# The gate projection of the last two token groups by seven block products instead of eight

## The chip, the cores and the metric

The kernel runs on one core of one Trainium2 chip. The metric is the device time of one execution in microseconds. Before the change it is 318.22 us, the median of 3 runs (317.78 to 318.86). The execution that was profiled took 317.96 us, of which the profile's span, from the first to the last instruction, is 316.2 us.

## The reference

A linear attention (cosformer) of 8 batches, 8 heads, 576 positions and 64 dimensions is followed by a gated feed-forward block. The attention's output, 4608 tokens of 512 values, is the input of three weight matrices. Cut to what matters:

```
q_p, k_p = phi(q), phi(k)              # relu, times cos and sin of the position
kv  = einsum('bhsf,bhsd->bhfd', k_p, v);  z = sum_s k_p
x   = (q_p @ kv) / (q_p . z + 1e-6)    # 4608 x 512 after the heads are joined
g   = x @ w_gate                       # 512 x 1536
val = x @ w_val                        # 512 x 1536
out = (g * sigmoid(g) * val) @ w_out   # 1536 x 512
```

All inputs and the output are float32 in memory. The kernel works in bfloat16 and float16 with float32 sums.

## The kernel before

**Groups and slots.** The 4608 tokens are 36 tiles of 128 and 9 groups (0 to 8) of 512 tokens. The order of all instructions is written out by hand; no scheduler moves them, and each engine takes its own list in order. The feed-forward work of a group is the frame. It has 16 slots: 12 columns of 128 gate and value outputs (`ffn_fc`, `fc` 0 to 11) and 4 steps of the output projection. Behind each step `slot(s)` issues what was planned for that slot with `at(s, ...)`: attention of the next group's tiles, work on the next batches' q, k and v, and their loads.

**A column before.** `ffn_mm` (L535) makes 4 matmuls of 512 columns with `wg_sb` into one PSUM bank and 4 with `wv_sb` into another. ScalarE takes the silu of the gate bank (`ffn_silu`, L541), VectorE multiplies it with the value bank into `ht` (`ffn_mul`, L546). `ht` holds 12 columns of 512 tokens in fp16.

**The output projection.** From group 2 on, `out_by_quarters` (matmuls at L649) computes `ht @ w_out` as a 2 x 2 block product by seven products for eight: `weight_sum` (L614) made four sums of `w_out` blocks once, in group 1; `token_sum` (L623) makes four sums of `ht` blocks in each group, called behind columns 7 to 11 (`sums_behind`). ScalarE seeds a bank with a copy (L671), later matmuls add to what was put there, and VectorE makes the sums between banks (L679, L690). Results go to `ob` (L662 on ScalarE, L664 on VectorE) and to memory by SP's queue (`store`, L574; in the last group `store_two`, L581, on two queues).

**PSUM.** All 8 banks are one tile. `take` picks a bank when the program is written: among those that nobody holds, the one that was touched longest ago. `give_back` ends a hold in the program's text; on the chip the next writer of the bank still waits by semaphore until the last reader is done. For `"o"` banks, one whose neighbour is held is preferred, so that pairs stay whole for the attention tiles, which need two.

**Attention of later tiles.** `a_tile2` (L419) makes 16 or 8 small matmuls per half tile into two banks; VectorE then makes den, rec and x (L429, L438, L442); `x_turn` transposes x into `xT` by a DMA on SP's queue (L519). `relu_k` and `phi_q` (L238, L255), `vmul` (L259) and `kv_mm` (L305) prepare the next batch. Loads of q, k, v and weights are issued by POOL (`load`, L111) behind small copies that hold the queue.

Of the kernel before, what the change touches and what calls it, by code (L numbers as in the profile page):

```python
# [10 lines left out]
FP32 = mybir.dt.float32  # L11
# [3 lines left out]
ALU = mybir.AluOpType  # L15
# [3 lines left out]
def kernel(  # L19
# [28 lines left out]
    HC = FC // 2  # L48
    HT = T // 2
    HD = d_model // 2  # L50

    consts = ctx.enter_context(tc.tile_pool(name="consts", bufs=1))
    raw = ctx.enter_context(tc.tile_pool(name="raw", bufs=3))
    rel = ctx.enter_context(tc.tile_pool(name="rel", bufs=1))
    phip = ctx.enter_context(tc.tile_pool(name="phip", bufs=2))
    xp = ctx.enter_context(tc.tile_pool(name="xp", bufs=4))
    xtp = ctx.enter_context(tc.tile_pool(name="xtp", bufs=3))
    smp = ctx.enter_context(tc.tile_pool(name="smp", bufs=3))
    sgp = ctx.enter_context(tc.tile_pool(name="sgp", bufs=5))
    obp = ctx.enter_context(tc.tile_pool(name="obp", bufs=2))  # L60
    psum = ctx.enter_context(tc.tile_pool(name="psum", bufs=1, space=bass.MemoryType.PSUM))

# [10 lines left out]
    def take(n, hold=None, fills=False, seeded=False):  # L73

        taken = {x for r in held.values() for x in r}
        free = [b for b in range(0, 8, n) if not any(b <= x < b + n for x in taken)
                and (filled[b] or not seeded)]

        b0 = min(free, key=lambda b: (n == 1 and hold is not None and hold[0] == "o" and b ^ 1 not in taken,
                                      sorted(used[b:b + n], reverse=True)))  # L80
        if hold is not None:
            held[hold] = range(b0, b0 + n)
        filled[b0:b0 + n] = [fills or seeded] * n
        touch(range(b0, b0 + n))
        return banks[:, b0] if n == 1 else banks[:, b0:b0 + n]
# [15 lines left out]

    def raw_of(b, nm):
        if (b, nm) not in raws:
            raws[b, nm] = raw.tile([P, G, NC, D], BF16, name=f"raw_{nm}")
        return raws[b, nm]

    def load(b, nm, parts=1):
# [48 lines left out]
    ident = consts.tile([P, P], BF16)  # L156
    make_identity(nc, ident)
    kvd = []
    for j in range(2):
        t = consts.tile([P, 8 * J * D1], BF16, name=f"kvd_{j}")  # L160
        if j:
            nc.gpsimd.memset(t.bitcast(FP32), 0.0)
        kvd.append(t.rearrange("p (e j w i x) -> p e j w i x", e=2, j=J, w=2, i=2))


    zeros = consts.tile([P, P], BF16)
# [41 lines left out]
        in_=csk.rearrange("p c e -> p (c e)").to_broadcast([P, NC * 2, D]),  # L208
    )
    v2s = []  # L210
    for j in range(2):
        t = consts.tile([P, G, NC, 2, W], BF16, name=f"v2_{j}")
        nc.vector.tensor_copy(out=t[:, :, :, :, D], in_=csk.unsqueeze(1).to_broadcast([P, G, NC, 2]))
        v2s.append(t)


    wg_sb = consts.tile([P, KC, d_ff], BF16)
    wv_sb = consts.tile([P, KC, d_ff], BF16)
    wg_r = moe_w_gate.rearrange("(c p) f -> p c f", p=P)
    wv_r = moe_w_val.rearrange("(c p) f -> p c f", p=P)  # L220
    wo_r = moe_w_out.rearrange("(c p) f -> p c f", p=P)
# [35 lines left out]

    def vmul(b, g):
        nc.vector.tensor_tensor(  # L259
            out=v2s[b % 2][:, g, :, :, 0:D],  # L260
            in0=(first if b == 0 and g == 0 else {"v": raw_of(b, "v")})["v"][:, g].unsqueeze(2).to_broadcast([P, NC, 2, D]),
            in1=tab, op=ALU.mult,
        )
# [34 lines left out]
    def kv_mm(b):  # L298
        ps = st[b, "kvps"] = take(2, ("kv", b))
        for j, c in [(j, c) for j in range(J) for c in range(NC)]:  # L300
            for i in range(2):
                for e in range(2):
                    es = slice(e * SH, (e + 1) * SH)
                    g = 2 * j + i
                    nc.tensor.matmul(  # L305
                        out=ps[i * D:(i + 1) * D, e, j * 2 * D1:(j + 1) * 2 * D1],
                        lhsT=raws[b, "k"][es, g, c],
                        rhs=v2s[b % 2][es, g, c, :, 0:D1],
                        start=(c == 0), stop=(c == NC - 1),
                    )  # L310

# [47 lines left out]
            give_back(("kvf", j))  # L359


    qf = consts.tile([P, 2, J, 2, D], BF16)
    qr = [lodge(4 * J * SH, BF16).rearrange("p (e j c s) -> p e j c s", e=2, j=J, c=2) for i in range(2)]
    qwT = [lodge(8 * J * SH, BF16).rearrange("p (w e j c s) -> p w e j c s", w=2, e=2, j=J, c=2) for i in range(2)]

# [68 lines left out]
    def x_rec(t, ps, ys=slice(0, 4)):  # L434
        if ys.start == 0:
            st["rec", t] = smp.tile([P, H, 1], FP32, name="rec")
            st["x", t] = xp.tile([P, d_model], BF16, name="x")
        nc.vector.reciprocal(out=st["rec", t].rearrange("p (e y) o -> p e y o", e=2)[:, :, ys],  # L438
                             in_=st["den", t].rearrange("p (e y) o -> p e y o", e=2)[:, :, ys])

# [40 lines left out]
    def x_norm(t):  # L481
        num = st.pop(("num", t)).rearrange("p j e (i x) -> p (j e i) x", i=2)
        den = smp.tile([P, H, 1], FP32, name="den")
        nc.vector.tensor_scalar(out=den, in0=num[:, :, D:D1], scalar1=1e-6, scalar2=DOWN,
                                op0=ALU.add, op1=ALU.mult)
        rec = smp.tile([P, H, 1], FP32, name="rec")
        nc.vector.reciprocal(out=rec, in_=den)
        x = xp.tile([P, d_model], BF16, name="x")
        for j in range(J):
            hs = slice(4 * j, 4 * j + 4)  # L490
            nc.vector.tensor_tensor(
                out=x[:, 4 * j * D:(4 * j + 4) * D].rearrange("p (i e d) -> p e i d", i=2, e=2),
                in0=num[:, hs, 0:D].rearrange("p (e i) d -> p e i d", e=2),
                in1=rec[:, hs].rearrange("p (e i) o -> p e i o", e=2).to_broadcast([P, 2, 2, D]), op=ALU.mult,
            )
        st["x", t] = x

    def xT_of(t):
        tg, off = divmod(t, GH // 2)
        if tg not in xT:  # L500
            xT[tg] = xtp.tile([P, GH // 2, KC, P], BF16, name="xT")
        return xT[tg][:, off]

    def x_turn_pe(t, ks=slice(0, KC)):
        ps = take(1, ("xt", t, ks.start)).bitcast(BF16).rearrange("p (k x) -> p k x", x=P)
        for kc in range(ks.start, ks.stop):
            nc.tensor.transpose(out=ps[:, kc], in_=st["x", t][:, kc * P:(kc + 1) * P], identity=ident)  # L507
        st["xt", t, ks.start] = ps[:, ks]

    def x_turned(t, eng, ks=slice(0, KC)):  # L510
# [40 lines left out]
    def ffn_act(*a):  # L551
        ffn_silu(*a)
        ffn_mul(*a)

    def ffn_fc(*a):

        ffn_mm(*a)
        ffn_act(*a)

    out_v = out.rearrange("(b p c) f -> b c p f", p=SH, c=NC)  # L560
    o_ps = {}
# [68 lines left out]
    def out_by_quarters(tg, slot_of):  # L630
# [60 lines left out]
        if last:  # L691
            store_two(t0 + 2, slice(HD, d_model))
        product(c, aq[:, 1, 1], T4, False)
        copied("dve", C21, c)
        free("c")
        if last:
            store_two(t0 + 2, slice(0, HD))
# [178 lines left out]
    for b in range(2, B):  # L876
        s0 = SLOTS * (b - 1)
        keng = "dve" if b == 2 else "act"
        steps = [lambda b=b, g=g: phi_q(b, g) for g in range(G)]
        steps += [lambda b=b, g=g: (relu_k(b, g, g + 1, keng), vmul(b, g)) for g in range(G)]  # L880
        if b == 2:
            fs, tq = [s0 + i for i in (0, 0, 1, 1, 4, 5, 5, 6)], (s0 + 2, s0 + 2)
        else:
            p0 = s0 - SLOTS
            fs, tq = [p0 + 12, p0 + 12] + [p0 + 11 + i for i in range(2, 8)], (p0 + 15, p0 + 16)
            if b == 3:
                fs, tq = [p0 + 12 + i for i in range(4)] + [s0 + 4, s0 + 4, s0 + 5, s0 + 5], (s0 + 2, s0 + 2)
            at(p0 + 3 if b < 5 else p0 + 1, lambda b=b: load_behind(b))
        tk = (s0 + 4, s0 + {2: 8, 3: 7}.get(b, 5))
        for s, f in zip(fs, steps):  # L890
            at(s, f)
        for e in range(2):
            at(tq[e], lambda b=b, e=e: qturn_dma(b, e))
        at(tk[-1], lambda b=b: kv_mm(b), lambda b=b: kv_out2(b))
        at(tk[-1] + 1, lambda b=b: kv_free(b))
    for t in range(2 * OUT, NTG * OUT):
        tg, i = divmod(t, OUT)
        s = SLOTS * (tg - 1) + (5 if tg > 2 else 4) + 2 * i
        if t == 2 * OUT:
            at(s, a_(t, 0))  # L900
            at(s + 1, a_(t, 1), turn(t))
        elif tg == 2:
            at((9, 10, 11)[i - 1] + SLOTS, lambda t=t: a_tile2(t), turn(t))
            if i == 2:
                at(11 + SLOTS, load_3)
        else:
            if t in (13, 14, 15):
                s = SLOTS * 2 + t - 4
            at(s, lambda t=t: a_tile2(t), turn(t))
    for tg in range(1, NTG):  # L910
        s0 = SLOTS * tg
        for fc in range(FC):
            ffn_fc(tg, fc)
            if tg > 1:
                sums_behind(fc)
            slot(s0 + fc)
        if tg > 1:
            out_by_quarters(tg, lambda i: slot(s0 + FC + i))
            continue
        for i in range(OUT):  # L920
            ffn_out(tg * OUT + i)
            weight_sum(i)
            slot(s0 + FC + i)
# [31 lines left out]
```

## Time and profile before

| | before |
|---|---|
| time, median of 3 runs | 318.22 us (317.78 to 318.86) |
| profiled execution | 317.96 us, span 316.2 us |
| granted TensorE clock | 1.000 |
| TensorE busy | 309.1 us, 98% |
| VectorE busy | 220.2 us, 70% |
| ScalarE busy | 134.1 us, 42% |
| GpSimd (POOL) busy | 35.5 us, 11% |
| group 7, gate and value columns with attention tiles | 250.6 to 272.3 us |
| group 7, output projection | 272.3 to 281.5 us |
| group 8, gate and value columns | 281.5 to 302.2 us |
| group 8, output projection | 302.2 to 311.4 us |

PE is the matmul part of TensorE, PEld its weight loads, DVE is VectorE, ACT ScalarE, SP the engine whose queue issues most transfers. A row of the instructions in order of time gives the start, the time that the merged rows cover, engine, line, operation, out<-in, shape and count, and in brackets the idle time before it and what ended it. A matmul's duration runs beyond the start of the next, as they are pipelined; the distance of starts is what a stream costs.

### The profile page before, as it was taken

The numbers are of one execution on the slowest core, as the hardware profiler recorded it, in microseconds if no ns is written. First come the engines' busy times: TensorE is split into PE (matmuls) and PEld (weight loads), VectorE is DVE, ScalarE is ACT, GpSimd is POOL, SyncE is SP. The second block draws the span as 40 slices with busy tenths as digits, with TensorE's granted clock in tenths as the row PEclk, the third lists the DMA queues.
The fourth block names the chain that finished last, engine by engine and source line by source line (L and its number), as shares of the span: only waits on it lengthen the run. The fifth ranks groups of instructions, "written<-read, shape, count | busy, mean of one in ns | idle before, by whom it ended". The sixth has DMA issues, their size and how long they took to land.

```text
span 316.2 us, 6614 instructions
## 1 busy us (share of the span) xinstructions
PE 309.1 (98%) x2624; PEld 182.7 (58%) x2624; DVE 220.2 (70%) x441; ACT 134.1 (42%) x245; POOL 35.5 (11%) x60
## 2 busy tenths in 40 slices
PE   8899999999999999999999999999999999999994
PEld 4596555455445485548554765477456745774473
DVE  7873777797658888597858785879578437743652
ACT  7554545753435354335433453344433133213330
POOL 6754102000201100030003000300000000000000
PEclk9999999999999999999999999999999999999999
DMA  7999999998796985979795979598951241133004
GB/s 259 220 198 197 206 205 139 226 130 110 140 225 88 175 116 135 129 80 197 148 142 75 200 149 145 72 199 134 157 77 35 58 93 23 39 69 72 2 0 133
DMA packets 74766, 41.06 MB, mean 130 GB/s; under 512 B 49904, under 2 KB 69872, under 8 KB 74736
## 3 DMA queue, kind: packets, MB, share of 16 engines
q1 hardware_dynamic: 51952, 22.55, 39.7%
q0 software_dynamic: 22192, 17.57, 37.1%
q10 hardware_dynamic: 592, 0.52, 0.5%
q8 instruction: 20, 0.33, 0.4%
q14 instruction: 10, 0.08, 0.1%
HBM read 37.75 MB, written 9.44 MB: 149 GB/s over the span
## 4 chain that ended last, share of the span: by engine, by line
PE 86%; DVE 6%; DMA 4%; ACT 2%; issue 1%; DVEq 0%; ACTq 0%
PE banks L535 57%; PE banks L649 15%; PE banks L592 6%; DMA xT<-x 4%; PE banks L305 3%; PE banks L419 2%; DVE ht L546 1%; DVE sums L623 1%; DVE x L442 1%; PE banks L465 1%; PE banks L401 1%; DVE v L259 1%; PE banks L172 1%; PE banks L345 0%; PE banks L507 0%
## 5 line engine op out<-in xcount | busy, mean ns | idle before, releaser
L541 ACT ACTIVATE sg<-banks 128x512 bf16<-128x512 f32 (+2 forms) x116 | 65.8, 568 | 118.7 <-PE banks L535 115.6
L535 PE MATMUL banks<-xT,wg_sb 128*128 128x512 bf16 (+2 forms) x464 | 111.3, 364 | 0.3 <-DMA xT<-x 0.2
L535 PE MATMUL banks<-xT,wv_sb 128*128 128x512 bf16 (+2 forms) x464 | 111.3, 364 | 0.0
L546 DVE TENSOR_TENSOR ht<-sg,banks 128x512 f16<-128x512 bf16 (+2 forms) x116 | 74.5, 648 | 52.2 <-PE banks L535 45.5
L535 PEld LDWEIGHTS <-wv_sb 128*128 128x128 bf16 x464 | 44.9, 98 | 48.7
L535 PEld LDWEIGHTS <-wg_sb 128*128 128x128 bf16 x464 | 43.0, 98 | 42.3 <-issue 0.4
L649 PEld LDWEIGHTS <-ht 128*128 128x128 f16 x336 | 32.4, 98 | 3.9
L649 PEld LDWEIGHTS <-sums 128*128 128x128 f16 x252 | 24.6, 98 | 3.6 <-issue 0.8
L259 DVE TENSOR_TENSOR v<-raw_v,tab 128x1152 bf16<-128x1152 bf16 x31 | 22.7, 751 | 0.3 <-ACT raw_v L712 0.3
L592 PE MATMUL banks<-wo_sb,ht 128*128 128x512 f16 x96 | 22.7, 379 | 0.0
L442 DVE TENSOR_TENSOR x<-banks,rec 128x512 bf16<-128x512 f32 (+1 forms) x32 | 21.6, 674 | 1.3 <-PE banks L401 0.3
L649 PE MATMUL banks<-wo_sb,ht 128*128 128x256 f16 x168 | 20.6, 273 | 0.0
L649 PE MATMUL banks<-wt_sb,sums 128*128 128x256 f16 x168 | 19.5, 273 | 0.0
L649 PE MATMUL banks<-wt_sb,ht 128*128 128x256 f16 x168 | 19.5, 273 | 0.0
L255 DVE TENSOR_TENSOR r_q<-raw_q,tab 128x1152 bf16<-128x1152 bf16 x24 | 17.6, 752 | 2.4 <-ACT raw_q L238 2.1
L238 ACT ACTIVATE raw_k<-raw_k 128x576 bf16<-128x576 bf16 (+1 forms) x25 | 17.0, 694 | 0.0
L861 POOL COPY hold<-phit 1x2 bf16<-1x2 bf16 x5 | 1.2, 234 | 130.4 <-DMA phit<-r_q 130.4
L623 DVE TENSOR_TENSOR sums<-ht 128x1024 f16<-128x1024 f16 (+1 forms) x28 | 15.5, 552 | 0.2
L238 ACT ACTIVATE raw_q<-raw_q 128x576 bf16<-128x576 bf16 x24 | 15.0, 674 | 0.0
L592 PEld LDWEIGHTS <-ht 128*128 128x128 f16 x96 | 9.1, 98 | 8.9 <-issue 0.2
L419 PEld LDWEIGHTS <-phit 128*128 128x128 bf16 (+1 forms) x240 | 10.0, 100 | 6.5 <-issue 1.3
L664 DVE TENSOR_SCALAR ob<-banks 128x512 f32<-128x512 f32 (+1 forms) x15 | 9.8, 656 | 4.4 <-PE banks L649 3.6
(98 smaller groups left out, 223.9 us busy)
## 6 DMA issues: line engine op xcount, KB each, us to landing
out_dram<-ob SPq DMA_DIRECT2D x67, 128.0 KB, 2.4
raw_k<-in_k_dram POOLq DMA_DIRECT2D x7, 576.0 KB, 9.0
raw_q<-in_q_dram POOLq DMA_DIRECT2D x6, 576.0 KB, 6.5
raw_v<-in_v_dram POOLq DMA_DIRECT2D x6, 576.0 KB, 11.7
wo_sb<-in_moe_w_out_dram POOLq DMA_DIRECT2D x3, 512.0 KB, 12.8
wg_sb<-in_moe_w_gate_dram POOLq DMA_DIRECT2D x5, 256.0 KB, 9.0
wv_sb<-in_moe_w_val_dram POOLq DMA_DIRECT2D x5, 256.0 KB, 9.3
wo_sb<-in_v_dram SPq DMA_DIRECT2D x2, 576.0 KB, 4.1
```

Of the source, the lines that this page charges most:

```text
L238: nc.scalar.activation(out=out, in_=in_, func=AF.Relu)
L255: nc.vector.tensor_tensor(out=st[b, "q"][:, g], in0=o.unsqueeze(2).to_broadcast([P, NC, 2, D]), in1=tab, op=ALU.mult)
L259: nc.vector.tensor_tensor(out=v2s[b % 2][:, g, :, :, 0:D], in0=(first if b == 0 and g == 0 else {"v": raw_of(b, "v")})["v"][:, g].unsqueez ...
L419: nc.tensor.matmul(out=ps[ms, e, g * D1:(g + 1) * D1], lhsT=phit[b][:, e, g, c:c + n].rearrange("p c s -> p (c s)"), rhs=kv2s[b % 2][:, e, ...
L442: nc.vector.tensor_tensor(out=st["x", t].rearrange("p (y e d) -> p e y d", e=2, d=D)[:, :, ys], in0=ps[:, :, 0:2 * J * D1].rearrange("p e ...
L535: nc.tensor.matmul(out=st["f", tg, fc, lo][i], lhsT=(wg_sb, wv_sb)[i][:, kc, fs], rhs=xT[tg][:, ts, kc], start=(kc == 0), stop=(kc == KC - 1))
L541: nc.scalar.activation(out=sg[:, 0:n], in_=st["f", tg, fc, lo][0], func=AF.Silu, scale=DOWN)
L546: nc.vector.tensor_tensor(out=ht[:, fc, r:r + n], in0=st.pop(("s", tg, fc, lo))[:, 0:n], in1=ps[1], op=ALU.mult)
L592: nc.tensor.matmul(out=o_ps[t], lhsT=ht[:, fc, r:r + P], rhs=wo_sb[:, fc], start=(fc == 0), stop=(fc == FC - 1))
L623: nc.vector.tensor_tensor(out=o[:, lo:hi], in0=x[:, lo:hi], in1=y[:, lo:hi], op=op)
L649: nc.tensor.matmul(out=to[i][:, 0] if len(to) == 2 else to[0][:, i], lhsT=a[:, kc, i * P:(i + 1) * P], rhs=b[:, kc], start=first and kc == ...
L664: nc.vector.tensor_single_scalar(out=o_, in_=p_, scalar=x, op=ALU.mult)
```

## The change

The gate projection of groups 7 and 8 is computed block by block, 2 x 2 blocks, with seven products for eight, in the same form as the output projection. For each third `u` of the columns (4 columns of 128) the blocks are two halves of the 512 inputs and two halves of the 512 tokens.

- `ffn_by_quarters` replaces the 12 columns of `ffn_fc` in groups 7 and 8. A block product is 4 matmuls of 256 columns (L608 of the changed kernel). ScalarE seeds bank b with a copy of bank a (L636), copies the product e to `m7` in SBUF (L640); VectorE makes c = m7 + b in a bank (L646) and m7 = m7 + b (L655); ScalarE takes four silus of half columns (L614). The value columns stay 4 matmuls of 512 (L620), each into a bank of its own, and VectorE multiplies them with the gates (L625). The order of the columns is 0, 2, 1, 3, 4, 6, 5, 7, 8, 10, 9, 11.
- Sums: `gate_weight_sum` makes four sums of `w_gate` blocks into `wgs_sb`, one at the end of groups 1, 2, 4 and 5; `x_sum` (L592) makes four sums of `xT` blocks in slots 14 and 15 before each of the two groups. The sums of `ht` are called at other places in these groups.
- `take` prefers a bank whose neighbour is held also for names "g" and "v", while fewer than three pairs are whole.
- x, `xT` and the gate and value weights are fp16 in place of bf16; there is a second identity for it, made on POOL.
- Room: k and v have two raw buffers each in place of three; `v2_1` and `qf` lie in `wgs_sb` and serve only batches 0 and 1, so later batches all use `v2_0`; both `kvd` lie in one tile, which later holds the sums of x.
- C21 of the output projection is copied by ScalarE in place of VectorE, in all groups. Group 8's attention tiles stand in slots 1, 2, 5 and 6 of group 7 in place of 5, 7, 9 and 11.

```diff
-    raw = ctx.enter_context(tc.tile_pool(name="raw", bufs=3))
+    raw = ctx.enter_context(tc.tile_pool(name="raw", bufs=2))
+    rawq = ctx.enter_context(tc.tile_pool(name="rawq", bufs=3))
...
-        b0 = min(free, key=lambda b: (n == 1 and hold is not None and hold[0] == "o" and b ^ 1 not in taken,
+        whole = sum(b not in taken and b + 1 not in taken for b in range(0, 8, 2))
+        b0 = min(free, key=lambda b: (n == 1 and hold is not None and b ^ 1 not in taken and
+                                      (hold[0] == "o" or hold[0] in "gv" and whole < 3),
                                       sorted(used[b:b + n], reverse=True)))
...
+    ident16 = consts.tile([P, P], FP16)
+    make_identity(nc, ident16)
...
-            out=v2s[b % 2][:, g, :, :, 0:D],
+            out=v2s[b == 1][:, g, :, :, 0:D],
...
+    def gate_weight_sum(n):
+        o, x, y, op = ((W1, A21, A22, ALU.add), (W2, W1, A11, ALU.subtract), (W3, A11, A21, ALU.subtract),
+                       (W4, A12, W2, ALU.subtract))[n]
+        nc.vector.tensor_tensor(out=o, in0=x, in1=y, op=op)
...
+    def x_sum(tg, n):
+        B11, B12, B21, B22 = x_parts(tg)
+        o, x, y = ((X1, B12, B11), (X2, B22, X1), (X3, B22, B12), (X4, B21, X2))[n]
+        nc.vector.tensor_tensor(out=o, in0=x, in1=y, op=ALU.subtract)
+
+    def ffn_by_quarters(tg, slot_of):
...
+        def product(to, u, a, x, first):
+            for i in range(2):
+                for c in range(KH):
+                    nc.tensor.matmul(out=to[:, i], lhsT=a[:, c, 2 * u + i], rhs=x[:, :, c],
+                                     start=first and i == 0 and c == 0, stop=c == KH - 1, skip_group_check=True)
...
+        def V(u, i, w):
+            fc = 4 * u + 2 * i + w
+            val[u, i, w] = take(1, ("v", tg, fc), fills=True)
...
+        for u in range(3):
+            a = bank("a", fills=True)
+            product(a, u, A11, B11, True)
+            b = bank("b", seeded=True)
+            nc.scalar.copy(out=b, in_=a)
+            e = bank("e", fills=True)
+            product(e, u, W3, X3, True)
+            m7 = m7p.tile([P, 2, HT], FP32, name="m7")
+            nc.scalar.copy(out=m7, in_=e)
+            free("e")
+            V(*((u - 1, 1, 1) if u else (u, 0, 0)))
+            done()
+            product(b, u, W2, X2, False)
+            c = bank("c", seeded=True)
+            nc.vector.tensor_tensor(out=c, in0=m7, in1=b, op=ALU.add)
+            product(a, u, A12, B21, False)
+            silu(u, 1, 0, a)
+            free("a")
+            if u:
+                mul(u - 1, 1, 1)
+            V(u, 0, 0) if u else V(u, 1, 0)
+            done()
+            product(b, u, W1, X1, False)
+            nc.vector.tensor_tensor(out=m7, in0=m7, in1=b, op=ALU.add)
+            silu(u, 0, 1, m7)
+            product(c, u, A22, X4, False)
+            silu(u, 0, 0, c)
+            free("c")
+            V(u, 1, 0) if u else V(u, 0, 1)
+            done()
+            if u == 2:
+                for n in (1, 2):
+                    token_sum(n, 0, 4)
+            mul(u, 0, 0)
+            mul(u, 1, 0)
+            if u == 2:
+                token_sum(3, 4, 6)
+            product(b, u, W4, B22, False)
+            silu(u, 1, 1, b)
+            free("b")
+            if u:
+                V(u, 0, 1)
+            mul(u, 0, 1)
+            if u:
+                done()
+                token_sum(*((3, 0, 4) if u == 1 else (4, 0, 4)))
+        V(2, 1, 1)
+        mul(2, 1, 1)
+        for n in (1, 2):
+            token_sum(n, 4, 6)
+        done()
...
-        copied("dve", C21, c)
+        copied("act", C21, c)
...
+    for n in range(4):
+        at(SLOTS * (1 + n * (GATE[0] - 1) // 4) + FC + 3, lambda n=n: gate_weight_sum(n))
+    for tg in GATE:
+        for n in range(4):
+            at(SLOTS * (tg - 1) + FC + (2, 2, 3, 3)[n], lambda tg=tg, n=(2, 0, 1, 3)[n]: x_sum(tg, n))
...
+            elif tg - 1 in GATE:
+                s = SLOTS * (tg - 1) + ((1, 2, 7, 9) if tg < 6 else (1, 2, 4, 7) if tg < 8 else (1, 2, 5, 6))[i]
...
+        if tg in GATE:
+            ffn_by_quarters(tg, lambda i: slot(s0 + i))
+        for fc in range(FC) if tg not in GATE else ():
```

## The prediction

> **What bounds the kernel now.** I read the page's busy times first, then the chain that ended last, then TensorE's waits, and last the instructions in order of time for the stretch that the change rewrites.
>
> ```profile
> span 316.2 us, 6614 instructions
> PE 309.1 (98%) x2624; PEld 182.7 (58%) x2624; DVE 220.2 (70%) x441; ACT 134.1 (42%) x245; POOL 35.5 (11%) x60
> ...
> PEclk9999999999999999999999999999999999999999
> ...
> PE 86%; DVE 6%; DMA 4%; ACT 2%; issue 1%; DVEq 0%; ACTq 0%
> ```
>
> TensorE is busy 98% of the span at full clock, and 86% of the last chain is TensorE. Its end in order of time:
>
> ```profile
> 272.52 9.17 PE banks L649 x84
> 281.69 20.72 PE banks L535 x96
> 302.41 9.18 PE banks L649 x84
> 311.61 0.42 DVE ob L664
> ```
>
> One group of the last two is 96 matmuls (20.72 us) and 84 output matmuls (9.18 us), back to back. Only 4.6 us of the span lie behind the last matmuls. So a matmul saved there is time saved, and a wait of TensorE there is time lost. The rows in order of time give all prices:
>
> ```profile
> 276.28 1.47 PE L649 MATMUL banks<-wo_sb,ht 128*128 128x256 f16 x12
> 276.55 0.70 DVE L679 SCALAR_TENSOR_TENSOR banks<-ob,banks 128x512 f32<-128x512 f32 x1 [1.48 <-PE banks L649]
> ...
> 277.59 2.78 PE L649 MATMUL banks<-wt_sb,ht 128*128 128x256 f16 x24
> 277.79 0.60 ACT L662 ACTIVATE ob<-banks 128x512 f32<-128x512 f32 x1 [2.02 <-PE banks L649]
> ...
> 283.25 1.03 PE L535 MATMUL banks<-xT,wg_sb 128*128 128x512 bf16 x4
> 283.52 0.69 DVE L546 TENSOR_TENSOR ht<-sg,banks 128x512 f16<-128x512 bf16 x1 [1.10 <-PE banks L535]
> ...
> 284.11 1.03 PE L535 MATMUL banks<-xT,wv_sb 128*128 128x512 bf16 x4
> 284.31 0.60 ACT L541 ACTIVATE sg<-banks 128x512 bf16<-128x512 f32 x1 [1.13 <-PE banks L535]
> ```
>
> Starts matter more than durations here. Four 512-column matmuls take 284.11 - 283.25 = 0.86 us (20.72 / 96 = 0.216 each); twelve of 256 columns take 277.59 - 276.28 = 1.31 (0.109 each). ScalarE starts 0.20 us after the slot of the last matmul it needs ends (284.31 - 284.11), VectorE 0.27 (283.52 - 283.25). A silu lasts 0.60, a product or sum with a PSUM operand 0.69. So whoever waits for a silu of a bank gets it 0.80 us after the matmuls.
>
> **What goes.** Per group the gate part is 48 matmuls of 512 columns now and 3 x 7 x 4 = 84 of 256 then; the value part stays 48. That is 48 x 0.216 = 10.37 against 84 x 0.109 = 9.16: 1.2 us a group, 2.4 us in all. LDWEIGHTS (98 ns) stay under 109 ns. [...]
>
> **What comes on other engines, and why most is free.** Weight sums: 4 x 0.95 (row of L614, same shape) on VectorE, each at the end of the output part of groups 1, 2, 4 and 5, 2 and more groups ahead of use; it has 30% idle. Token sums of x: 4 x 0.42 a group (row of L623, 128x512). The first two run right after the output's C22 sum (L690, ends 279.79), where C21's copy stood, so X3 is there at 280.2 and needed 0.44 us after 281.52; their x tiles landed 2.4 us after an issue at 275.10. X1 and X2 come early too. C21's copy on ScalarE costs 0.60 where ScalarE waits 2 us (L662). Group 8's attention tiles move up from slots 5, 7, 9, 11 to 1, 2, 5, 6 with their transposes on SP's queue, which is empty there between 257 and 263 us. The extra identity on POOL, about 0.5 us by its rows (194 and 293 ns), stands before a copy that waits 1.8 us for the first v load, so POOL's queue of loads is not later. Two buffers for k and v: the load of k at 102.73 would reuse what the k/v products from 70.00 on read, 31 us earlier. One v2 tile: batch 3's writes, near 97 us, follow products that end at 71.2. fp16 for bf16: the fp16 output matmuls run at the same 0.216 (10.36 / 48 at L592). If that cover were gone: the weight sums cost up to 3.8, POOL 0.5, C21 0.6.
>
> **What comes on the path: the value matmuls' banks.** In the old loop a pair of banks comes round after four columns, some 7 us, and nobody waits. In the new one the choice of a bank changes: while fewer than three pairs are whole, a gate or value tile takes a bank whose neighbour is held. Right after `free("a")` that is bank a itself, whose silu has just been asked for, and after `free("c")` it is c. The value matmul behind it then waits for that silu, and all of TensorE behind it. Nothing in the trace of before shows this wait, but its parts are rows. I number time from group 7's first gate matmul, with 0.44 for a block product, 0.86 for a value column, 0.27 for an attention tile (8 small matmuls; 260.96 to 261.22 in this trace).
>
> Group 7, first third. Products a 0 to 0.44, e to 0.87, value column 0 to 1.74, b to 2.17, a to 2.61. Silu of a 2.81 to 3.41. Column 2 wants bank a: waits 3.41 - 2.61 = **0.80**, and ends 4.27. Attention tile to 4.54, b to 4.98, c to 5.41. VectorE takes the tile's three operations (rows 0.16, 0.20, 0.69) from 4.81 to 5.91 before it can do m7 + b, to 6.6; then silu of m7 to 7.2 and, behind it in ScalarE's queue, silu of c to 7.83. Column 1 wants bank c at 5.41: waits **2.4**.
> Second third. Column 1 ends 8.7, tile, b, a and e end 10.27. Column 3 gets the bank of column 1, whose multiplication is the last of three behind another tile's x: x ends 10.3, the three end 10.9, 11.6, 12.2. Waits **1.9**. Column 4 wants bank a again: **0.80**. Columns 6 and 5 find multiplied banks.
> Last third. Column 7 takes the bank of column 5: tile x, then three multiplications on VectorE, TensorE waits **0.75**. Columns 8 to 11 find free banks. In the output part the last two sums of ht stand behind this backlog: **0.4**. Small rest 0.1.
> Sum 0.80 + 2.4 + 1.9 + 0.80 + 0.75 + 0.5 = 7.2.
>
> Group 8 has no attention tiles. Column 2 **0.80**. Column 1 without the tile on either engine: c ends 1.3 after column 2, m7 + b ends 1.4 after b's 0.44 and 0.27 + 0.69, two silus (0.66 and 0.60) end 2.67 after column 2 and c is done at 0.87: **1.8**. Columns 4 and 8 behind silu of a: **0.80** each. Output part, last copies and sums behind multiplications: **0.4**. Sum 4.6.
>
> The bounds of the whole, if the waits are there at all (A below is the case without them): from below, each of the five waits for silu of a cannot be under 0.60, and the four others are between 0.7 (a single silu or multiplication, never less, as the bank's reader follows by program order) and the sums above: 3.0 + 2.8 = 5.8. From above, every such wait lengthened by the largest queue seen (one silu and one multiplication, 1.3): 11.8 + 4 x 1.3 = 17. I take 11.8, since each of its terms is a chain of rows of this trace. Net: 11.8 - 2.4 = +9.4 us.
>
> The profiled execution took 317.96 us (span 316.2 and 1.8 around it), 0.3 below the median of 318.22. 317.96 + 9.4 = **327.3 us**, 2.9% slower.
>
> **The clock.** It is full in every slice, so the trace shows no price for a pause. [...]
>
> **The rivals.**
> A, faster: the change does just what it says, 317.96 - 2.4 = 315.5 us. Mechanism: the value columns' banks are ready when TensorE comes. Place: the column behind silu of a. It decides from where 0.80 us of other TensorE work stand between the last product into the bank and the column that reuses it. For it: ScalarE is only 42% busy and could answer at once. Against: in the order of the code nothing stands between. Chance 0.04.
> B, half the waits: only the 0.80s and single links of the long chains are paid (5.8 to 9), because VectorE's queue is shorter than I count. 317.96 - 2.4 + 7.4 = 323. For it: VectorE's streams overlap by some 0.06 us at each start. Chance 0.17.
> C, longer still: a longer queue at nearly three of the four long waits (1.3 each, 3.5), 317.96 - 2.4 + 11.8 + 3.5 = 331 us. For it: group 7 chains ScalarE and VectorE three times over; against it: both have room, 42% and 70% busy. Chance 0.13.
> D, the saving is not paid by waits but lost elsewhere, say the loads of k and v with two buffers late in groups 2 to 6 while the waits are hidden: 318 within 0.3%. Against: the 31 us above. Chance 0.02.
> My forecast: 0.64.
>
> **How the numbers follow.** 327.3 is the forecast's; its own range is 325 to 329.5 (one long wait more or less). From B's 323 to C's middle holds 8 in 10: 323.5 to 330.5. A measurement here tells 0.3% (about 1 us) from no change. Faster by more: A, 0.04. Within it: D, 0.02. Slower: forecast, B and C, 0.94.
>
> **What will show it.** Right: TensorE's waits, all but empty behind 60 us now, gain value-column matmuls waiting for the silu (about 8 us in seven waits, the longest near 2.4 and 1.8 us) and for the multiplication into ht (two, near 1.9 and 0.75); block products stand 0.109 us apart; group 7's gate and value part is 19.5 + 6.7 us without its tiles, and everything before 250 us is as it was. Wrong: if those columns start right behind the matmuls before them, or if TensorE's start of group 7 has moved by more than 0.5 us.

## The result and the profile after

The changed kernel takes 326.38 us, the median of 4 runs (326.18 to 327.39); the kernel before took 318.54 us beside it (4 runs, 317.78 to 318.92). The ratio is 1.0256, with a 95% interval of 1.0225 to 1.0286: slower by 2.6%. The forecast was 327.3 us. The profiled execution is the longest of the four, 327.39 us with a span of 325.6; why it stands 1 us above the other three is a finding of its own, below.

The page of the changed kernel, the same lines as were read before the change:

```profile
span 325.6 us, 6776 instructions
PE 310.1 (95%) x2696; PEld 190.4 (58%) x2696; DVE 228.7 (70%) x458; ACT 143.8 (44%) x264; POOL 35.7 (11%) x62
...
PEclk9999999999999999999999999999999899999998
...
PE 85%; DVE 8%; ACT 3%; DMA 2%; issue 1%; DVEq 0%; ACTq 0%
```

TensorE's busy time is about what it was (310.1 us for 309.1), but its share fell from 98% to 95%. So it is not more work that makes the kernel longer; TensorE stands still where it did not before. Two slices show an 8 in the granted clock: one in the middle of the stretch that the change rewrites, and the last, behind the last matmul, where it costs nothing. VectorE and ScalarE gained 8.5 and 9.7 us of busy time and stay at 70% and 44%: neither is a bound by its share.

The chain that ended last, in order of time, of its longest pieces those at the end (start, time, engine, what, how many):

```profile
258.22 1.67 PE banks L620 x4
261.50 1.80 DVE ht L625 x3
270.62 1.29 DVE ht L625 x2
...
295.78 1.31 PE banks L608 x12
310.07 1.73 PE banks L620 x8
311.79 9.32 PE banks L773 x84
```

Before, one matmul line followed another here without a break. Now VectorE's multiplications into `ht` (L625) stand between the matmuls. TensorE's waits of the changed kernel (what waits, on what, us in total, times, the longest) name what is waited for, silus and multiplications:

```profile
PE banks L620 <- ACT sg L614: 7.1, 7, 2.1
PE banks L620 <- DVE ht L625: 1.4, 2, 0.9
```

Neither line exists in the kernel before. The instructions in order of time for group 7's first third show how one such wait comes about, and then the long one:

```profile
252.70 0.60 PE L608 MATMUL banks<-xT,wg_sb 128*128 128x256 f16 x4
...
253.33 0.60 ACT L614 ACTIVATE sg<-banks 128x512 bf16<-128x512 f32 x1 [1.10 <-PE banks L608]
253.98 1.02 PE L620 MATMUL banks<-xT,wv_sb 128*128 128x512 f16 x4 [0.69 <-ACT sg L614]
...
255.74 0.69 DVE L458 TENSOR_TENSOR x<-banks,rec 128x512 f16<-128x512 f32 x1
...
256.35 0.68 DVE L655 TENSOR_TENSOR m<-m,banks 128x512 f32<-128x512 f32 x1
...
257.06 0.63 ACT L614 ACTIVATE sg<-m 128x512 bf16<-128x512 f32 x1 [3.12 <-DVE m L655]
257.59 0.58 ACT L614 ACTIVATE sg<-banks 128x512 bf16<-128x512 f32 x1
258.22 1.67 PE L620 MATMUL banks<-xT,wv_sb 128*128 128x512 f16 x4 [2.09 <-ACT sg L614]
```

The second product into bank a starts at 252.70 and its four matmuls take 0.44, to 253.14. Silu of a starts at 253.33, ends at 253.93, and value column 2, which was given bank a, starts at 253.98: 0.84 us late. Column 1 then waits behind a chain: the attention tile's x (255.74), the sum m7 + b (256.35), silu of m7 (257.06), silu of c (257.59).

The idle time in brackets counts from the modelled end of the last matmul. What a wait costs is a little more: the distance from one start to the next, less the matmuls in between at 0.216 us (512 columns), 0.109 (256) and 0.033 (attention tiles). By that measure, and in us, the waits of the changed kernel's profile are

| place | worked out before | measured |
|---|---|---|
| group 7, column 2 (silu of a) | 0.80 | 0.84 |
| group 7, column 1 (silu of c) | 2.4 | 2.24 |
| group 7, column 3 (multiplication) | 1.9 | 1.07 |
| group 7, column 4 (silu of a) | 0.80 | 0.85 |
| group 7, column 7 (multiplication) | 0.75 | 0.65 |
| group 7, output part | 0.4 | 0.25 |
| group 8, column 2 | 0.80 | 0.84 |
| group 8, column 1 | 1.8 | 1.71 |
| group 8, columns 4 and 8 | 1.6 | 1.69 |
| group 8, output part | 0.4 | 0.14 |
| the rest | 0.1 | 0.1 |
| sum | 11.8 | 10.4 |

Another 1.6 us are lost without any wait. Behind the 2.09 us pause the matmuls of 512 columns soon start 0.43 us apart and no longer 0.216 (column 1's four start at 258.22, 258.44, 258.83 and 259.25, and the next instruction at 259.68). The table of windows (start and end in us, length, then busy time and instructions of PE, PEld, DVE, ACT and POOL, the granted clock, the DMA share and GB/s) shows why:

```profile
256.00:257.00 1.00, 0.14 (x2) 0.00 (x0) 1.00 (x2) 0.00 (x0) 0.00 (x0) 1.00 0.29 59
257.00:258.00 1.00, 0.00 (x0) 0.00 (x0) 0.02 (x1) 0.94 (x2) 0.00 (x0) 1.00 0.34 73
258.00:259.00 1.00, 0.78 (x3) 0.36 (x3) 0.00 (x0) 0.17 (x1) 0.00 (x0) 0.73 0.35 68
259.00:260.00 1.00, 1.00 (x9) 0.47 (x7) 0.00 (x0) 0.00 (x0) 0.00 (x0) 0.50 0.00 0
260.00:261.00 1.00, 1.00 (x11) 0.75 (x9) 0.57 (x3) 0.00 (x0) 0.00 (x0) 0.50 0.00 0
261.00:262.00 1.00, 1.00 (x7) 0.74 (x6) 1.00 (x2) 0.60 (x1) 0.00 (x0) 0.56 0.00 0
```

TensorE was granted half its clock for 3.42 us (0.54 in the third row, 1 and 1, and 0.88 in the last). The account of the spans closes: 10.4 + 1.6 - 2.4 saved = 9.6, against 325.6 - 316.2 = 9.4 measured. Group 7's first gate matmul starts at 250.52 us, 250.60 before, so all of it lies behind 250 us.

### The profile page after: what moved, and what is told of

Same layout as the page of the kernel before. It is cut to its first block, busy times and chain, and to the rows that moved or that the text cites. A ratio compares the mean times of both kernels' runs of the same rounds, so it can differ in the third digit from the quotient of the medians.

```text
span 325.6 us, 6776 instructions
## 1 busy us (share of the span) xinstructions
PE 310.1 (95%) x2696; PEld 190.4 (58%) x2696; DVE 228.7 (70%) x458; ACT 143.8 (44%) x264; POOL 35.7 (11%) x62
## 4 chain that ended last, share of the span: by engine, by line
PE 85%; DVE 8%; ACT 3%; DMA 2%; issue 1%; DVEq 0%; ACTq 0%
PE banks L551 44%; PE banks L773 16%; PE banks L716 6%; PE banks L620 6%; PE banks L608 4%; PE banks L320 3%; PE banks L435 2%; DMA xT<-x 2%; DVE ht L625 2%; ACT sg L614 2%; DVE sums L747 1%; DVE x L458 1%; PE banks L481 1%; PE banks L417 1%; DVE v L274 1%
## 5 line engine op out<-in xcount | busy, mean ns | idle before, releaser
L551 PE MATMUL banks<-xT,wg_sb 128*128 128x512 f16 (+2 forms) x368 | 86.6, 360 | 0.2 <-DMA xT<-x 0.2
L551 PE MATMUL banks<-xT,wv_sb 128*128 128x512 f16 (+2 forms) x368 | 86.6, 360 | 0.0
L557 ACT ACTIVATE sg<-banks 128x512 bf16<-128x512 f32 (+2 forms) x92 | 51.5, 560 | 76.2 <-PE banks L551 74.2
L562 DVE TENSOR_TENSOR ht<-sg,banks 128x512 f16<-128x512 bf16 (+2 forms) x92 | 57.9, 637 | 30.0 <-PE banks L551 22.8
L551 PEld LDWEIGHTS <-wv_sb 128*128 128x128 f16 x368 | 35.5, 98 | 37.4
L551 PEld LDWEIGHTS <-wg_sb 128*128 128x128 f16 x368 | 33.9, 98 | 31.8 <-issue 0.5
L620 PE MATMUL banks<-xT,wv_sb 128*128 128x512 f16 x96 | 24.9, 386 | 8.4 <-ACT sg L614 7.1
L458 DVE TENSOR_TENSOR x<-banks,rec 128x512 f16<-128x512 f32 (+1 forms) x32 | 21.6, 674 | 1.3 <-PE banks L417 0.3
L620 PEld LDWEIGHTS <-wv_sb 128*128 128x128 f16 x96 | 9.4, 98 | 16.7 <-issue 10.3
L625 DVE TENSOR_TENSOR ht<-sg,banks 128x512 f16<-128x512 bf16 x24 | 15.6, 680 | 3.4 <-ACT sg L614 3.3
L614 ACT ACTIVATE sg<-banks 128x512 bf16<-128x512 f32 x18 | 10.3, 591 | 12.6 <-PE banks L608 12.5
```

Source lines behind the costliest of these rows:

```text
L458: nc.vector.tensor_tensor(out=st["x", t].rearrange("p (y e d) -> p e y d", e=2, d=D)[:, :, ys], in0=ps[:, :, 0:2 * J * D1].rearrange("p e ...
L551: nc.tensor.matmul(out=st["f", tg, fc, lo][i], lhsT=(wg_sb, wv_sb)[i][:, kc, fs], rhs=xT[tg][:, ts, kc], start=(kc == 0), stop=(kc == KC - 1))
L557: nc.scalar.activation(out=sg[:, 0:n], in_=st["f", tg, fc, lo][0], func=AF.Silu, scale=DOWN)
L562: nc.vector.tensor_tensor(out=ht[:, fc, r:r + n], in0=st.pop(("s", tg, fc, lo))[:, 0:n], in1=ps[1], op=ALU.mult)
L620: nc.tensor.matmul(out=val[u, i, w], lhsT=wv_sb[:, kc, fc * P:(fc + 1) * P], rhs=xT[tg][:, :, kc], start=(kc == 0), stop=(kc == KC - 1))
L625: nc.vector.tensor_tensor(out=ht[:, fc], in0=gates[u, w][:, i], in1=val.pop((u, i, w)), op=ALU.mult)
```

## The experiments

The theory: the saving of 2.4 us is there, and the loss is paid at the value columns, because `take` gives them a bank whose silu has only just been asked for. The first rival: ScalarE and VectorE are too slow for the new order of the work, whichever bank is taken. The second: the loss lies in the other parts (two buffers for k and v, weight sums, C21 on ScalarE, moved tiles). A later question was what brings the clock down. All kernels are the changed kernel with the edit shown; none leaves part of the computation out.

**e1: the old choice of a bank.**

```diff
-        b0 = min(free, key=lambda b: (n == 1 and hold is not None and b ^ 1 not in taken and
-                                      (hold[0] == "o" or hold[0] in "gv" and whole < 3),
+        b0 = min(free, key=lambda b: (n == 1 and hold is not None and b ^ 1 not in taken and hold[0] == "o",
                                       sorted(used[b:b + n], reverse=True)))
```

> The changed kernel with one line put back: a gate or value bank is again the one that was touched longest ago, with no preference for one whose neighbour is held. Theory (the bank): the value columns no longer take a bank just released, so of the 10.3 us of waits only about 1.8 us of VectorE's queue stay, and the 2.4 us of fewer columns show: 318.5 - 2.4 + 1.8 = about 317.9 us, 8 us below the changed kernel, and no wait of a value column for a silu. Rival (the engines): ScalarE and VectorE are too slow for seven products in any bank, TensorE waits elsewhere: 324 to 327 us.

Measured: 316.58 us (6 runs, 316.24 to 317.26), ratio to the kernel before 0.9943 (0.9926 to 0.9960). The two wait lines of L620 are gone. TensorE's waits of this kernel, all of them (its lines are numbered one lower from `take` on):

```profile
PE banks L183 <- DVE zeros L178: 1.0, 1, 1.0
PE banks L391 <- DVE wgs_sb L383: 0.7, 1, 0.7
PE banks L416 <- DVE wt_sb L404: 0.6, 1, 0.6
PE banks L607 <- DVE x L457: 0.3, 1, 0.3
```

The first three lie at the start of the kernel. The same third as above, TensorE alone:

```profile
252.34 0.60 PE L607 MATMUL banks<-xT,wg_sb 128*128 128x256 f16 x4
252.78 1.03 PE L619 MATMUL banks<-xT,wv_sb 128*128 128x512 f16 x4
...
254.33 0.60 PE L607 MATMUL banks<-kvt,wg_sb 128*128 128x256 f16 x4
254.77 1.03 PE L619 MATMUL banks<-xT,wv_sb 128*128 128x512 f16 x4
```

Both columns start 0.44 us after the product before them, with no idle time. ScalarE, VectorE and the order of all instructions are the same; only bank numbers differ. So the rival of slow engines falls: one expression in `take` is worth 9.8 us, and with it put back the change makes the kernel faster than before, by 0.6%. What is still lost in the two groups is 1.26 us, the largest piece 0.51 where a gate bank waits for an attention tile's x.

**e2: e1, and a sum of ht moved.** The fourth sum of `ht` moves behind the last first and second sums, so that the output part finds them earlier.

```diff
-                token_sum(*((3, 0, 4) if u == 1 else (4, 0, 4)))
+            if u == 1:
+                token_sum(3, 0, 4)
...
             token_sum(n, 4, 6)
+        token_sum(4, 0, 4)
```

> As e1_lru, and the sum S4 of ht, which is needed last, stands behind the last S1 and S2 in place of ahead of them. Theory (the bank): the wait in the output part (about 0.4 us a group) goes too: 0.8 us below e1_lru, about 317.1 us, below the kernel before by 1.4. Rival (the engines): no better than 324 us.

Measured: 316.54 us (6 runs, 316.20 to 317.05), ratio 0.9942 (0.9925 to 0.9959). The two waits in the output parts (0.22 and 0.14 us in e1) are gone, but the time is the same as e1's. The expected gain was too large, and executions of one kernel differ by more than those 0.36 us.

**e3: all of the change but the block products.**

```diff
-    GATE = (7, 8)
+    GATE = ()
...
-        at(SLOTS * (1 + n * (GATE[0] - 1) // 4) + FC + 3, lambda n=n: gate_weight_sum(n))
+        at(SLOTS * (1 + n * (7 - 1) // 4) + FC + 3, lambda n=n: gate_weight_sum(n))
```

The weight sums are still made; groups 7 and 8 run the old columns, without sums of x, and group 8's tiles fall back to their old slots.

> The changed kernel with no group by seven products: fp16, two raw buffers, one v2 tile, weight sums and C21 on ScalarE stay. Theory (the bank): all of the loss lies in the two groups, so 318.5 us, within 0.5 of the kernel before. Rival (the rest): if sums, buffers or fp16 cost what was put down to waits, 320 to 326 us.

Measured: 317.89 us (10 runs, 317.72 to 318.47), ratio 0.9984 (0.9973 to 0.9996). The weight sums, fp16, the smaller buffers, the second identity and C21 on ScalarE cost nothing together; if anything they gain 0.5 us, for which this study has no explanation. The second rival falls for these parts. The sums of x and the moved tiles are not in e3; e1 has both, and its gain leaves no room for a cost of theirs. TensorE loses nothing in the last two groups of this kernel, so 317.89 us is the base on which the rest can be counted.

**e4: block products in group 8 alone.** As e3, with `GATE = (8,)`.

> The changed kernel with seven products in group 8 alone, with its attention tiles at their old slots in group 7. Theory (the bank): group 8's waits of about 4.5 us less 1.2 us saved: 318.5 + 3.3 = 321.8 us; group 7 as before. Rival (the engines, VectorE's attention work): group 8 has none of it, so it would gain 1.2 us: 317.3 us.

Measured: 320.87 us (4 runs, 320.74 to 321.32), ratio 1.0080 (1.0060 to 1.0099). Group 8 shows its waits without group 7's backlog of attention tiles; TensorE in order of time:

```profile
284.87 1.02 PE L620 MATMUL banks<-xT,wv_sb 128*128 128x512 f16 x4 [0.69 <-ACT sg L614]
...
288.25 1.02 PE L620 MATMUL banks<-xT,wv_sb 128*128 128x512 f16 x4 [1.49 <-ACT sg L614]
...
293.01 1.02 PE L620 MATMUL banks<-xT,wv_sb 128*128 128x512 f16 x4 [0.68 <-ACT sg L614]
...
297.77 0.60 PE L608 MATMUL banks<-kvt,wgs_sb 128*128 128x256 f16 x4 [0.27 <-DVE ht L625]
```

Columns 2, 1 and 4 lose 0.85, 1.65 and 0.85 us, as in the full change; all losses come to 4.1 us. Each group pays for itself.

**e9: the preference for the gate banks alone.** `hold[0] in "gv"` becomes `hold[0] in "g"`, so a value column takes the bank touched longest ago.

> The preference for a bank with a held neighbour is kept for the gate part's banks (a, b, c, e) alone and taken away from the value columns. Theory (the value columns' taking of the bank just released is what costs): the seven waits for silu go, what is left are banks of the gate part that come back early, some 2 to 4 us in all: 319 to 320.5 us. Rival (any use of the preference makes the waits, whichever tile has it): 324 to 326.4 us.

Measured: 319.24 us (11 runs, 318.84 to 319.83), ratio 1.0027 (1.0013 to 1.0040). The value columns wait no more. What is left, of TensorE's waits:

```profile
PE banks L608 <- DVE ht L625: 2.0, 2, 1.1
...
PE banks L435 <- ACT sg L614: 0.5, 1, 0.5
```

Now gate products wait for a multiplication and an attention tile for a silu, 3.7 us lost in all. So of the 9.8 us that the preference costs, some 7.1 go when the value columns give it up and the other 2.7 when the gate banks do so too.

**e6: the sum m7 + b ahead of the attention tile.** VectorE takes the three operations of the tile after the sum, not before it.

```diff
             V(u, 0, 0) if u else V(u, 1, 0)
-            done()
             product(b, u, W1, X1, False)
             nc.vector.tensor_tensor(out=m7, in0=m7, in1=b, op=ALU.add)
             silu(u, 0, 1, m7)
+            done()
```

> Isolates one link of the longest chain: VectorE's three operations of the attention tile now stand behind m7 + b. Theory (column 1 of group 7 waits for c's silu, which stands behind m7's silu, which stands behind VectorE's queue): its start comes 2.24 us late in the changed kernel; without the tile ahead the chain is that of group 8, 1.71 late there, and the tile's 0.27 us of matmuls no longer hide a part of it but come behind the products: 1.4 to 1.7 us late. The rest stays, so 0.5 to 0.9 us are gained: 325.5 to 325.9 us. Rival (the wait is only ScalarE's, two silus behind one another, VectorE plays no part): unchanged, 326.4.

Measured: 325.92 us (4 runs, 325.56 to 326.11), ratio 1.0225 (1.0202 to 1.0248). VectorE, ScalarE and TensorE around column 1:

```profile
255.72 0.69 DVE L654 TENSOR_TENSOR m<-m,banks 128x512 f32<-128x512 f32 x1 [1.82 <-PE banks L608]
...
256.44 0.63 ACT L614 ACTIVATE sg<-m 128x512 bf16<-128x512 f32 x1 [2.27 <-DVE m L654]
...
256.97 0.58 ACT L614 ACTIVATE sg<-banks 128x512 bf16<-128x512 f32 x1
...
257.60 1.02 PE L620 MATMUL banks<-xT,wv_sb 128*128 128x512 f16 x4 [1.23 <-ACT sg L614]
...
258.92 0.17 DVE L445 TENSOR_SCALAR den<-banks 128x8 f32<-128x8 f32 x1 [1.48 <-PE banks L435]
...
259.97 1.87 DVE L625 TENSOR_TENSOR ht<-sg,banks 128x512 f16<-128x512 bf16 x3
...
261.89 0.38 PE L620 MATMUL banks<-xT,wv_sb 128*128 128x512 f16 x1 [1.70 <-DVE ht L625]
```

Column 1 is 1.39 us late, not 2.24, as expected: 0.85 of it came from VectorE's queue. The time falls by less, 0.5 us. Column 3 does not explain the rest: it is 1.85 us late here (1.70 in brackets), starting 4.29 us after column 1, but the tile that was moved has no part in that, as VectorE had finished it and stood idle for 1.48 us before the next tile's den (258.92). The same work lies between the two columns in the changed kernel. That column 3 was only 1.07 late in its profile is because the matmuls ahead of it ran at half clock and came to it later. The 0.4 us that the median does not show are less than e6's own executions differ by (325.56 to 326.11); where they went is not shown.

**r_after, e8 and e10: the length of the pause and the clock.** r_after is the changed kernel again. In e8 the silu of m7 in group 7's first third is done twice, in e10 four times, each time with the same values; this only lengthens the pause before column 1.

```diff
             silu(u, 0, 1, m7)
+            if tg == 7 and u == 0:
+                silu(u, 0, 1, m7)
```

> The changed kernel itself once more, with many executions, for the clock. In the one profiled execution TensorE was granted half clock from 258.5 to 261.9 us, right behind the pause of 2.1 us before column 1 of group 7, and its mean clock was 0.991; its other executions had 0.997 to 1.000 and were about 1 us shorter. If the pause brings the clock down only now and then, most executions here are near 326.3 us at 0.997 or above, and any at 0.992 or below are about 1 us longer. If the half clock of the profile had another cause (a start that varies), time and clock are not tied together.

> The silu of m7 is done twice in the first third of group 7 (the same values, written twice), so ScalarE's queue before silu of c is one silu of 0.60 us longer. Theory: column 1 starts 2.8 to 2.9 us late for 2.24, everything behind it shifts, 326.4 + 0.6 = 327.0 us while the clock stays. The pause is then some 2.7 us; if its length is what halves the clock (2.1 us did it in one execution of four), half clock comes in most executions: listed clock 0.992 or below and about 1 us more on top, 328 us. Rival (time of column 1 is set elsewhere): 326.4.

> The silu of m7 is done four times in the first third of group 7 (the same values each time), three more than in the changed kernel. Column 1 should start 2.24 + 3 x 0.6 = 4.0 us late, and all of it is paid: 326.4 + 1.8 = 328.2 us at full clock. The pause is then some 3.9 us, longer than the 3.42 us for which the half clock lasted in three profiles. [...] If the pause's length has no part in it: half clock in less than half of them.

| kernel | pause shown before column 1, us | executions: us at mean granted clock | median, us |
|---|---|---|---|
| e6 | 1.23 | 325.89 at 0.997, 325.96 at 1.000, 325.56 at 0.996, 326.11 at 0.999 | 325.92 |
| changed, first runs | 2.09 | **327.39 at 0.991**, 326.18 at 0.997, 326.43 at 1.000, 326.33 at 0.997 | 326.38 |
| changed, r_after | 2.09 | **326.90 at 0.993**, 326.88 at 1.000, **326.82 at 0.993**, **327.41 at 0.991**, 326.38 at 1.000 | 326.88 |
| e8 | 2.75 | **328.01 at 0.992**, 327.35 at 1.000, 327.06 at 1.000, **328.29 at 0.995**, 327.02 at 1.000 | 327.35 |
| e10 | 4.07 | **329.38 at 0.991**, **329.50 at 0.991**, **329.47 at 0.995**, **329.53 at 0.988**, **329.13 at 0.991** | 329.47 |

Bold are the executions at 0.995 or below. 3.42 us at half clock take 1.7 / 326 = 0.5% off the mean. The clock falls again behind the last matmul; that takes up to 2.3 us of the span in these profiles (323.31 to 325.6 in the changed kernel's first), 0.4% of the mean, so 0.996 and above are read as full clock up to the last matmul. The ratios to the kernel before are 1.0256 (1.0232 to 1.0280) for r_after, 1.0277 (1.0254 to 1.0301) for e8 and 1.0339 (1.0314 to 1.0365) for e10. TensorE's wait and the windows behind it in e10:

```profile
260.27 1.59 PE L620 MATMUL banks<-xT,wv_sb 128*128 128x512 f16 x4 [4.07 <-ACT sg L614]
```

```profile
260.00:261.00 1.00, 0.73 (x3) 0.34 (x3) 0.00 (x0) 0.22 (x1) 0.00 (x0) 0.79 0.00 0
261.00:262.00 1.00, 1.00 (x9) 0.49 (x7) 0.00 (x0) 0.00 (x0) 0.00 (x0) 0.50 0.00 0
262.00:263.00 1.00, 1.00 (x11) 0.75 (x9) 0.59 (x3) 0.00 (x0) 0.00 (x0) 0.50 0.00 0
263.00:264.00 1.00, 1.00 (x6) 0.71 (x5) 1.00 (x3) 0.60 (x1) 0.00 (x0) 0.50 0.00 0
```

The half clock lasts 0.42 + 3 = 3.42 us here too, and 3.42 in the profiles of r_after and e8. Time and clock go together, though not in every single execution (one of 326.88 has full clock): the changed kernel's four with half clock average 327.13 us, the other five 326.44. In r_after they were three of five, more than expected. Half clock comes in none of 4 executions of e6, 4 of 9 of the changed kernel, 2 of 5 of e8 and all 5 of e10. The expectation for e8 (half clock in most) was wrong, its time right; e10's time lies 1.3 us above the 328.2 that its expectation works out at full clock. So the half clock goes with the pause: it came in none of the executions with 1.23 us and in every one with 4.07, while for pauses of 2.09 and 2.75 us something that differs from execution to execution decides.

What that is, no run shows. The pause's length alone does not give the moment at which the clock falls. In the changed kernel's first profile it falls 0.24 us after column 1's start (258.46 behind 258.22), in r_after's 1.06 us after it (259.40 behind 258.34). Behind the last matmul of the first profile (its end is at 321.10 us) the clock falls after 2.2 us (323.31); in the kernel before TensorE stands still for 4.6 us there, to the end of the span, and the clock is still full.

**The account over all runs.** Base is e3's median, 317.89 us. Each line takes off 1.2 us for each group with block products and adds everything that its profile shows as lost in the last two groups, waits and slow matmuls together:

| kernel | lost, us | 317.89 - saved + lost | profiled execution | median |
|---|---|---|---|---|
| e2 | 0.9 | 316.4 | 316.89 | 316.54 |
| e1 | 1.3 | 316.8 | 316.27 | 316.58 |
| e9 | 3.7 | 319.2 | 319.62 | 319.24 |
| e4 | 4.1 | 320.8 | 320.74 | 320.87 |
| e6 | 10.2 | 325.7 | 325.89 | 325.92 |
| r_after | 11.2 | 326.7 | 326.90 | 326.88 |
| changed | 12.0 | 327.5 | 327.39 | 326.38 |
| e8 | 12.5 | 328.0 | 328.01 | 327.35 |
| e10 | 13.9 | 329.4 | 329.38 | 329.47 |

Every row agrees with the profiled execution within 0.5 us, over a range of 13 us; that is no more than executions of one kernel differ. Saving and lost time explain all runs. Lost time and profiled time come from the same execution, so this is bookkeeping: it shows that nothing outside the two groups moved by more than 0.5 us. (The medians of the changed kernel and of e8 lie lower than their profiled executions because those two had half clock.)

At full clock the changed kernel was not profiled, but two estimates give what it lost there. By its executions, 326.44 - 317.89 + 2.4 = 10.95 us; the waits other than column 3's are 9.3 of it in both profiles, which leaves 1.6 for column 3. By e6's rows, where column 3 starts 4.29 us after column 1 at full clock, column 3 is 1.85 late and all come to 11.15. The 0.2 between them are less than executions differ by.

## Why the prediction was right

**The saving, 2.4 us.** Right. Products of 256 columns start 0.109 us apart (four in 0.44 us) and e1 shows the gain once the waits are gone: 317.89 - 316.58 = 1.3, plus the 1.26 still lost, is 2.6.

**What was costed at nothing.** Right within the measurement: weight sums, sums of x, C21 on ScalarE, fp16, the smaller buffers and the moved tiles show no wait of TensorE in the two groups, and e3, which has all of these but the sums of x and the moved tiles, is 0.5 us below the kernel before, not above.

**The waits for silu of a, 0.80 each.** Right: 0.84 and 0.85, five times. The 0.04 missing lies between the end of silu and the start of the matmul (253.93 to 253.98 in the rows above).

**The long chains.** Columns 1 came at 2.24 for 2.4 and 1.71 for 1.8; VectorE's operations overlap a little at their starts (x at 255.74 for 0.69, the sum already at 256.35). e6 took VectorE's link out alone, and column 1 came 0.85 us earlier. Column 3, at full clock, 1.6 by the executions and 1.85 by e6's rows, for 1.9. Column 7: 0.65 for 0.75. In group 8 the working has c end 1.3 us after column 2; that is a slip, two products take 0.87, which is the number it goes on with. That these waits come from the choice of the bank is what e1 shows.

**The mis-sized terms.** The waits of the output parts, 0.25 and 0.14 us for 0.4 each, and the four long chains, together 0.4 to 0.6 too long; the five short waits were 0.2 too short. So 10.95 to 11.15 us at full clock stand against 11.8, and that is most of the 0.9 by which the forecast of 327.3 lies above the median of 326.38.

**What the forecast left out: the clock.** The sum of 11.8 has no term for it; the trace of the kernel before shows a full clock in every slice. In the changed kernel it fell in four of nine executions, behind a wait of 2.1 us. The slow matmuls cost 1.6 us in the first profile; in r_after's it was 0.8, since there the clock fell at 259.40, when column 1's matmuls were through (258.34 to 259.20). But column 3 waits for VectorE in any case, so part of it is hidden: slow matmuls and column 3's wait together are 2.7 us in the first profile and 1.9 in r_after's, against 1.85 in e6 at full clock. On average the times differ by 0.7. That this did no harm to the forecast was luck, as three of the first four runs had full clock; in r_after only two of five had, with a median of 326.88.

**The rivals.** A, 315.5 us if the banks were ready, describes e1: 316.58, within 1.1 us. Its condition was named correctly (0.80 us of other work between the last product and the column that reuses its bank), and the changed kernel does not meet it. B, C and D did not come.

## What to carry to other kernels

Giving a buffer back in the program's text is not the same as having it free: for each reuse, add up what the last reader still has in front of it in its own queue, and compare that with the work that stands between. A rule that packs tiles closely into few banks (here to keep pairs whole) can pick the bank that was released last, and then costs TensorE the reader's full latency (0.84 to 0.85 us at each of the five silus of a here); the plain choice of the bank touched longest ago turned a loss of 2.6% into a gain of 0.6% with everything else the same. When a change saves in principle and loses on the chip, count the lost starts of the bounding engine first: here saving and lost time alone gave every run within 0.5 us.

## What the runs showed of the hardware

After a pause of TensorE the granted clock can fall to half. Behind pauses of 2.09 us it fell to 0.50 for 3.42 us in 4 of 9 executions (two of them profiled, the others by their mean clock), behind 2.75 us in 2 of 5 and behind 4.07 us in 5 of 5, and in none of e6's 4, where that pause is 1.23 us and the longest in the two groups 1.70. The half clock began 0.2 to 1.1 us after the matmuls had started again (at 258.46 behind 258.22 in the changed kernel's first profile, at 259.40 behind 258.34 in r_after's), so the matmuls behind the pause start at full speed and slow down afterwards: column 1's first two stand 0.22 us apart in the first profile and the later ones 0.39 to 0.43, and in r_after's all four take 0.86 us (258.34 to 259.20).
